# Decode attention with a gated MLP on one core: two heads side by side on the partitions, a packed P·V, and a new order of the loads

## The chip, the core and the metric

The kernel runs on one core of a Trainium2 chip (trn2). Time is device microseconds of one execution; a kernel's figure is the median of its fast runs. An execution also has a *span*, from its first to its last instruction. In nearly every run the time is some 1.8 us longer than the span (363.06 against 361.3).

## The reference, cut to what matters

```python
# B = 2 sequences, one new token each; 32 heads of 128; 4096 cached keys and values a head
q = x @ wq                                        # [2, 4096]
p = softmax(q . k_cache / sqrt(128))              # per sequence and head, over 4096 keys
o = p @ v_cache                                   # k_cache and v_cache: 67 MB each
a = o @ wo                                        # [2, 512]
b = relu(x_B @ w1) @ w2                           # w1 [512, 1376], w2 [1376, 512]
g = sigmoid((x * gate_w).sum(-1))
return g * a + (1 - g) * b
```

Every value of both caches is read once and used in two operations, so nearly all of the 145 MB that the kernel loads are K and V.

## The kernel before

The work goes in 32 steps, a step being two neighbouring heads of one sequence. A K tile has 128 partitions, and each partition holds 32 keys of the first head and then 32 of the second: two runs of 8 KB. A tile lies in SBUF, the on-chip memory. VectorE (DVE) multiplies the tile with q, TensorE (PE) sums the products in 16 matmuls with the identity, DVE finishes the sum, ScalarE (ACT) takes the exponential, and PE multiplies with V.

```python
def load_k(s):                                    # load_v is alike
    t = kpool.tile([P, 2, NC, Dh], bf16, name="kt")           # NC = 32
    nc.sync.dma_start(out=t, in_=A_k_cache[b, h : h + 2].rearrange("h (p c) d -> p h c d", p=P))
...
def pv(s):                                        # 32 matmuls, 2 output rows, 256 columns
    for c in range(NC):
        nc.tensor.matmul(o_ps, lhsT=PT_sb[:, c, 2 * s : 2 * s + 2], rhs=vt[:, :, c, :], ...)
...
def epi(s):                                       # scale, two transposes, and for b = 1 two matmuls with wo
    ...
for s in range(NP + 2):                           # NP = 32
    if s < NP: mult(s)
    if s >= 2: epi(s - 2)
    if s < NP: red(s)
    if 1 <= s <= NP: scores(s - 1); pv(s - 1)
    if s == 14: mlp()
    ...                                           # wq, wo (by quarters), w1 at s = 5, w2 at s = 7
    load_k(s + 3)
    load_v(s + 2)
res = g * a_ps + b2                               # then one output load
```

The softmax here doesn't subtract the row's maximum and nothing guards it: scores larger than these inputs give would overflow.

## Time and profile before

| | before |
|---|---|
| time, median (15 runs) | 363.59 us (361.99 to 365.68) |
| profiled run: time, span | 366.02 us, 364.2 us |
| loaded | 145.43 MB in 24,628 packets of the load queue |
| PE / DVE / ACT busy | 286.8 / 168.1 / 48.3 us |

### The profile page before, as it was taken

The page shows a single profiled execution, that of the slowest core. Times are in us where ns is not written, and L with a number is a line of the kernel's source. Part 1 is how long each engine was busy: PE and PEld are TensorE (multiplying, and loading weights), DVE is VectorE, ACT ScalarE, POOL GpSimd, SP SyncE. Part 2 cuts the span into 40 slices and gives each one's busy share as a digit, 9 for nine tenths or more (in the row PEclk, how much of TensorE's full clock was granted, in tenths as well). Part 3 has the DMA queues.
Part 4 walks back from the last instruction along what each step waited for, and adds up shares of the span by engine and source line. Part 5 has one row for each costly group of instructions (what it writes and reads, how often), then busy time and mean ns, then how long its engine had stood idle before and what let it go on. Part 6 is the DMA issues. An engine that isn't in the chain of part 4 may idle for free.

```text
span 364.2 us, 4195 instructions
## 1 busy us (share of the span) xinstructions
PE 286.8 (79%) x1812; PEld 152.6 (42%) x1815; DVE 168.1 (46%) x106; ACT 48.3 (13%) x212; POOL 0.7 (0%) x6
## 2 busy tenths in 40 slices
PE   0597977697888498469958989988979989958895
PEld 0143544253444154325614455544424455524443
DVE  0565551455451555135065555555505556455500
ACT  1201110012111011001021111111021111111011
POOL 0000000000000000000000000000000000000000
PEclk9988988699999699969899999999899999989989
DMA  7999999999999999999999999999999999999920
GB/s 253 426 426 428 429 407 426 430 426 427 427 431 405 426 426 410 429 426 427 426 428 420 404 420 417 401 427 428 426 430 426 425 428 425 416 427 425 421 94 0
DMA packets 24927, 145.70 MB, mean 400 GB/s; under 512 B 1511, under 2 KB 5709, under 8 KB 8525
## 3 DMA queue, kind: packets, MB, share of 16 engines
q1 hardware_dynamic: 24628, 145.43, 96.0%
q8 instruction: 14, 0.23, 0.2%
q10 hardware_dynamic: 280, 0.01, 0.0%
q14 instruction: 5, 0.03, 0.0%
HBM read 145.43 MB, written 0.00 MB: 399 GB/s over the span
## 4 chain that ended last, share of the span: by engine, by line
PE 40%; DMA 38%; DVE 16%; ACT 3%; SPq 1%; issue 1%; DVEq 0%; ACTq 0%
DMA kt<-in_A_k_cache_dram 38%; PE red L178 22%; DVE prod L171 15%; PE o_ps L211 11%; PE mm L153 2%; PE a_ps L233 2%; ACT qb L160 1%; ACT o L223 1%; PE mm L287 1%; PE mm L273 1%; PE gs L202 1%; PE tr L226 1%; ACT OT_sb L229 0%; SPq L320 0%; SPq L324 0%
## 5 line engine op out<-in xcount | busy, mean ns | idle before, releaser
L171 DVE TENSOR_TENSOR prod<-kt,qb 128x8192 bf16<-128x8192 bf16 x32 | 141.5, 4421 | 37.1 <-DMA kt<-in_A_k_cache_dram 36.7
L178 PE MATMUL red<-prod,ident 128*128 128x512 bf16 x512 | 131.2, 416 | 33.3 <-DVE prod L171 33.3
L211 PE MATMUL o_ps<-vt,PT_sb 128*2 128x256 bf16 x1024 | 116.9, 272 | 0.0
L178 PEld LDWEIGHTS <-ident 128*128 128x128 bf16 x512 | 52.8, 105 | 104.7 <-issue 60.1
L211 PEld LDWEIGHTS <-PT_sb 128*2 128x2 bf16 x1024 | 83.9, 84 | 24.3
L206 DVE RECIPROCAL rsg<-gs 2x1 f32<-2x1 f32 x32 | 5.0, 155 | 137.8 <-PE gs L202 137.8
L223 ACT ACTIVATE o<-o_ps,rsg 2x256 bf16<-2x256 f32 x32 | 14.8, 464 | 191.4 <-PE o_ps L211 191.4
L153 PE MATMUL mm<-wq,xb 128*128 128x512 bf16 x61 | 17.5, 403 | 17.3 <-DMA wq<-in_A_wq_dram 8.2
L192 ACT ACTIVATE PT_sb<-sc 128x32 bf16<-128x32 f32 x64 | 17.8, 338 | 54.7 <-DVE sc L190 54.7
L190 DVE TENSOR_REDUCE sc<-red 128x64 f32<-128x512 f32 x32 | 21.8, 681 | 0.6 <-PE red L178 0.6
L226 PE MATMUL tr<-ident,o 2*128 2x2 bf16 x64 | 6.3, 165 | 19.6 <-ACT o L223 19.6
L153 PEld LDWEIGHTS <-xb 128*128 128x128 bf16 x64 | 6.3, 101 | 27.5 <-issue 19.2
L226 PEld LDWEIGHTS <-o 2*128 2x128 bf16 x64 | 3.5, 92 | 29.5 <-ACT o L223 29.5
L160 ACT CAST qb<-mm 128x512 bf16<-128x512 f32 x16 | 9.4, 585 | 42.9 <-PE mm L153 42.9
L192 ACT ACTIVATION_READ_ACCUMULATOR PT_sb<-sc 128x1 f32 x64 | 13.5, 212 | 0.0
L233 PE MATMUL a_ps<-wo,OT_sb 128*2 128x512 bf16 x32 | 9.5, 377 | 4.0 <-ACT OT_sb L229 4.0
L202 PEld LDWEIGHTS gs<-ones_col,partials 128*2 128x2 f32 x64 | 2.8, 82 | 13.5 <-issue 13.1
L229 ACT COPY OT_sb<-tr 128x2 bf16<-128x2 bf16 x32 | 5.2, 163 | 9.3 <-PE tr L226 9.3
L202 PE MATMUL gs<-ones_col,partials 128*2 128x1 f32 x64 | 6.1, 164 | 0.0
L294 DVE TENSOR_SCALAR b<-mm,omg 2x512 f32<-2x512 f32 x1 | 0.7, 737 | 10.5 <-PE mm L287 10.5
L287 PE MATMUL mm<-w_sb,hT 128*2 128x512 bf16 (+1 forms) x11 | 4.2, 562 | 0.3 <-ACT hT L282 0.3
L233 PEld LDWEIGHTS <-OT_sb 128*2 128x2 bf16 x32 | 1.4, 81 | 5.5 <-ACT OT_sb L229 5.5
(21 smaller groups left out, 12.0 us busy)
## 6 DMA issues: line engine op xcount, KB each, us to landing
kt<-in_A_k_cache_dram SPq DMA_DIRECT2D x32, 2048.0 KB, 22.8
vt<-in_A_v_cache_dram SPq DMA_DIRECT2D x31, 2048.0 KB, 22.2
wq<-in_A_wq_dram SPq DMA_DIRECT2D x4, 1024.0 KB, 14.0
wo<-in_A_wo_dram SPq DMA_DIRECT2D x4, 1024.0 KB, 19.4
w_sb<-in_B_w_dram SPq DMA_DIRECT2D x1, 1376.0 KB, 28.9
w_sb<-in_B_w_dram SPq DMA_DIRECT2D x1, 1280.0 KB
vt<-in_A_v_cache_dram SPq DMA_DIRECT2D x1, 1024.0 KB, 14.6
vt<-in_A_v_cache_dram SPq DMA_DIRECT2D x2, 512.0 KB, 15.9
```

Of the source, the lines that this page charges most:

```text
L153: nc.tensor.matmul(ps, lhsT=xb[:, b, c, :], rhs=wq[:, c, n0 : n0 + 512], start=(c == 0), stop=(c == DC - 1),)
L160: nc.scalar.copy(out=qb[:, b, n0 : n0 + 512], in_=ps)
L171: nc.vector.tensor_tensor(out=prod, in0=kt, in1=q, op=ALU.mult)
L178: nc.tensor.matmul(ps, lhsT=ident, rhs=prod[:, :, j * RW : (j + 1) * RW], start=(j == 0), stop=(j == Dh // RW - 1),)
L190: nc.vector.reduce_sum(out=sc, in_=ps, axis=AX.X)
L192: nc.scalar.activation(out=PT_sb[:, :, 2 * s + i], in_=sc[:, i * NC : (i + 1) * NC], func=ACT.Exp, scale=inv_sqrt_dh, accum_out=partials[: ...
L202: nc.tensor.matmul(gs, lhsT=partials[:, 2 * s : 2 * s + 2], rhs=ones_col, start=True, stop=True)
L211: nc.tensor.matmul(o_ps, lhsT=PT_sb[:, c, 2 * s : 2 * s + 2], rhs=vt[:, :, c, :], start=(c == 0), stop=(c == NC - 1),)
L223: nc.scalar.activation(out=o4, in_=o_t.pop(s), func=ACT.Copy, scale=rsg_t.pop(s))
L226: nc.tensor.transpose(tr[:, 2 * i : 2 * i + 2], o4[:, i * Dh : (i + 1) * Dh], ident[:2, :2])
L233: nc.tensor.matmul(a_ps, lhsT=OT_sb[:, hh, :], rhs=wo[:, hh - g * GH, :], start=(hh == 0), stop=(hh == H - 1),)
L287: nc.tensor.matmul(b_ps, lhsT=hT[:fs, fc, :], rhs=w2_sb[:fs, fc, :], start=(fc == 0), stop=(fc == FC - 1),)
```

## The change

Its intent: larger pieces for the load engines, fewer and wider matmuls for P·V, and loads at the very end that nothing long has to wait for. The two heads of a step now lie side by side on the partitions (64 each), so a partition holds 64 keys of one head, one run of 16 KB. Four chunks of 128 values go into one P·V matmul with 8 output rows, and four small matmuls with a selection matrix combine them. K is loaded two steps ahead of V where it was one, the first K comes ahead of wq, and the last quarter of wo and all of w2 come last. The gate is now multiplied in earlier, so that attention and MLP add up in one accumulator, `a_ps`.

```diff
-        t = kpool.tile([P, 2, NC, Dh], bf16, name="kt")
-            out=t, in_=A_k_cache[b, h : h + 2].rearrange("h (p c) d -> p h c d", p=P)
+        return cache[b, h : h + 2].rearrange("h (p c) d -> (h p) c d", p=HP)      # kv_view, HP = 64
+        t = kpool.tile([P, NC, Dh], bf16, name="kt")                              # NC = 64
+        nc.sync.dma_start(out=t, in_=kv_view(A_k_cache, s))
...                                               # wo in 8 KB rows, wq in two loads of 4 KB rows
-        for c in range(NC):
-            nc.tensor.matmul(o_ps, lhsT=PT_sb[:, c, 2 * s : 2 * s + 2], rhs=vt[:, :, c, :], ...)
+        for q in range(NQ):                       # NQ = 16, JB = 4
+            nc.tensor.matmul(o_ps, lhsT=PT_sb[:, s % PT_SLOTS, q * JB : (q + 1) * JB, :] ...,
+                             rhs=vt[:, q * JB : (q + 1) * JB, :], ...)
...                                               # sums, evac, comb, unpack, wo_mm in place of epi
+        if 2 <= s < NP + 2:
+            pv(s - 2)
+        if s == NP + 2:
+            mlp_o()                               # the MLP's 11 output matmuls, into the same a_ps
...
-        load_v(s + 2)
+        load_v(s + 1)
+        if s + 1 == NP - 1:
+            load_wo(NG - 1)
+            load_w2()
```

More of the change, by code (lines that the diff above doesn't have):

```diff
@@ L17 @@
 RW = 8
+JB = 4
+PT_SLOTS = 4
 @with_exitstack
@@ L45 @@
     P = nc.NUM_PARTITIONS
+    HP = P // 2
     assert Dh == P
     DC = D // P
-    NC = Sk // P
-    BH = B * H
-    NP = BH // 2
+    NC = Sk // HP
+    NQ = NC // JB
+    M = 2 * JB
+    NP = B * H // 2
     NG = H // GH
-    PPG = B * GH // 2
+    GP = GH // 2
+    PPG = B * GP
+    DR = GH * Dh // P
+    DA = Dh // DR
+    WQG = 2
     inv_sqrt_dh = 1.0 / (float(Dh) ** 0.5)
@@ L59, in pair @@
         g, r = divmod(s, PPG)
-        b, r = divmod(r, GH // 2)
-        return g, b, g * GH + 2 * r
+        b, i = divmod(r, GP)
+        return g, b, i
     consts = ctx.enter_context(tc.tile_pool(name="consts", bufs=1))
@@ L69 @@
     qbpool = ctx.enter_context(tc.tile_pool(name="qbpool", bufs=2))
-    smalls = ctx.enter_context(tc.tile_pool(name="smalls", bufs=4))
+    smalls = ctx.enter_context(tc.tile_pool(name="smalls", bufs=3))
     PS = bass.MemoryType.PSUM
@@ L74 @@
     mmp = ctx.enter_context(tc.tile_pool(name="mmp", bufs=1, space=PS))
-    trp = ctx.enter_context(tc.tile_pool(name="trp", bufs=1, space=PS))
+    combp = ctx.enter_context(tc.tile_pool(name="combp", bufs=1, space=PS))
     gsp = ctx.enter_context(tc.tile_pool(name="gsp", bufs=1, space=PS))
@@ L81, with load_wq, kv_view @@
     wq_view = A_wq.rearrange("(p c) n -> p c n", c=DC)
-    wo_view = A_wo.rearrange("(h p) j -> p h j", p=P)
     wq_t, qb_t, wo_t, k_t, v_t = {}, {}, {}, {}, {}
-    def load_wq(g):
-        t = wqpool.tile([P, DC, GH * Dh], bf16, name="wq")
-        nc.sync.dma_start(out=t, in_=wq_view[:, :, g * GH * Dh : (g + 1) * GH * Dh])
-        wq_t[g] = t
-    def load_wo(g):
-        t = wopool.tile([P, GH, D], bf16, name="wo")
-        nc.sync.dma_start(out=t, in_=wo_view[:, g * GH : (g + 1) * GH, :])
+    def load_wq(i):
+        w = WQG * GH * Dh
+        t = wqpool.tile([P, DC, w], bf16, name="wq")
+        nc.sync.dma_start(out=t, in_=wq_view[:, :, i * w : (i + 1) * w])
+        wq_t[i] = t
+    def load_wo(g):
+        t = wopool.tile([P, DR, D], bf16, name="wo")
+        rows = GH * Dh
+        nc.sync.dma_start(
+            out=t, in_=A_wo[g * rows : (g + 1) * rows].rearrange("(p r) j -> p r j", r=DR)
+        )
         wo_t[g] = t
+    def kv_view(cache, s):
+        g, b, i = pair(s)
+        h = g * GH + 2 * i
+        return cache[b, h : h + 2].rearrange("h (p c) d -> (h p) c d", p=HP)
     def load_k(s):
@@ L98, in load_k @@
             return
-        _, b, h = pair(s)
-        t = kpool.tile([P, 2, NC, Dh], bf16, name="kt")
-        nc.sync.dma_start(
-            out=t, in_=A_k_cache[b, h : h + 2].rearrange("h (p c) d -> p h c d", p=P)
-        )
+        t = kpool.tile([P, NC, Dh], bf16, name="kt")
+        nc.sync.dma_start(out=t, in_=kv_view(A_k_cache, s))
         k_t[s] = t
@@ L108, in load_v @@
             return
-        _, b, h = pair(s)
-        t = vpool.tile([P, 2, NC, Dh], bf16, name="vt")
-        view = A_v_cache[b, h : h + 2].rearrange("h (p c) d -> p h c d", p=P)
-        cuts = [0, NC] if s < NP - 1 else [0, NC // 2, 3 * NC // 4, NC]
+        t = vpool.tile([P, NC, Dh], bf16, name="vt")
+        view = kv_view(A_v_cache, s)
+        cuts = [0, NC] if s < NP - 1 else [0, NC // 2, NC]
         for c0, c1 in zip(cuts, cuts[1:]):
-            nc.sync.dma_start(out=t[:, :, c0:c1, :], in_=view[:, :, c0:c1, :])
+            nc.sync.dma_start(out=t[:, c0:c1, :], in_=view[:, c0:c1, :])
@@ L115, in load_v @@
         v_t[s] = t
+    pad = consts.tile([P, 32], bf16, name="pad")
+    nc.gpsimd.memset(pad, 0.0)
+    load_k(0)
     xT = consts.tile([P, B, DC], bf16, name="xT")
-    nc.scalar.dma_start(out=xT, in_=A_x[:, 0, :].rearrange("b (p c) -> p b c", c=DC))
+    nc.sync.dma_start(out=xT, in_=A_x[:, 0, :].rearrange("b (p c) -> p b c", c=DC))
+    gwT = consts.tile([P, DC], bf16, name="gwT")
+    nc.sync.dma_start(out=gwT, in_=gate_w.rearrange("(p c) -> p c", c=DC))
     load_wq(0)
-    x_sb = consts.tile([B, D], bf16, name="x_sb")
@@ L121 @@
-    nc.scalar.dma_start(out=x_sb, in_=A_x[:, 0, :])
-    gw_sb = consts.tile([B, D], bf16, name="gw_sb")
-    nc.scalar.dma_start(out=gw_sb, in_=gate_w.partition_broadcast(B))
-    load_k(0)
     load_k(1)
+    load_k(2)
     load_v(0)
-    load_k(2)
-    load_v(1)
     ident = consts.tile([P, P], bf16, name="ident")
     make_identity(nc, ident[:])
-    ones_col = consts.tile([P, 1], fp32, name="ones_col")
-    nc.vector.memset(ones_col, 1.0)
-    PT_sb = consts.tile([P, NC, BH], bf16, name="PT_sb")
@@ L135 @@
-    partials = consts.tile([P, BH], fp32, name="partials")
-    OT_sb = consts.tile([P, H, B], bf16, name="OT_sb")
+    sel = consts.tile([M, JB, 32], bf16, name="sel")
+    nc.gpsimd.memset(sel, 0.0)
+    nc.gpsimd.affine_select(
+        out=sel,
+        in_=sel,
+        compare_op=ALU.not_equal,
+        fill=1.0,
+        base=0,
+        pattern=[[-2, JB], [-1, 2], [0, DA]],
+        channel_multiplier=1,
+    )
+    half = consts.tile([P, M], fp32, name="half")
+    nc.vector.memset(half, 0.0)
@@ L137 @@
+    nc.vector.memset(half[:HP, 0::2], 1.0)
+    nc.vector.memset(half[HP:, 1::2], 1.0)
+    PT_sb = consts.tile([P, PT_SLOTS, NC, 2], bf16, name="PT_sb")
+    nc.vector.memset(PT_sb, 0.0)
+    umask = consts.tile([P, DA], fp32, name="umask")
+    nc.vector.reduce_sum(
+        out=umask, in_=ident.rearrange("p (k a) -> p a k", a=DA), axis=AX.X
+    )
+    partials = consts.tile([P, NP], fp32, name="partials")
+    OT_sb = consts.tile([P, NG, DR, B], bf16, name="OT_sb")
     w1_sb = consts.tile([P, DC, Dff], bf16, name="w1_sb")
@@ L138 @@
     w2_sb = consts.tile([P, FC, D], bf16, name="w2_sb")
-    xb = consts.tile([P, B, DC, P], bf16, name="xb")
+    xb = consts.tile([P, B, DC, HP], bf16, name="xb")
     for b in range(B):
         nc.vector.tensor_copy(
-            out=xb[:, b], in_=xT[:, b, :].unsqueeze(2).to_broadcast([P, DC, P])
+            out=xb[:, b], in_=xT[:, b, :].unsqueeze(2).to_broadcast([P, DC, HP])
         )
+    gwb = consts.tile([P, DC, P], bf16, name="gwb")
+    nc.vector.tensor_copy(out=gwb, in_=gwT.unsqueeze(2).to_broadcast([P, DC, P]))
@@ L144 @@
     a_ps = apool.tile([B, D], fp32, name="a_ps")
+    g_sb = consts.tile([P, B], fp32, name="g_sb")
+    omg = consts.tile([P, B], fp32, name="omg")
     def make_qb(g):
-        wq = wq_t.pop(g)
-        qb = qbpool.tile([P, B, GH * Dh], bf16, name="qb")
+        wq = wq_t[g // WQG].rearrange("p c (i t d) -> p c t i d", t=2, d=Dh)
+        i0 = (g % WQG) * GP
+        qb = qbpool.tile([P, B, GP, Dh], bf16, name="qb")
         for b in range(B):
-            for n0 in range(0, GH * Dh, 512):
-                ps = mmp.tile([P, 512], fp32, name="mm")
+            ps = mmp.tile([P, GP * Dh], fp32, name="mm")
+            for t in range(2):
@@ L152, in make_qb @@
                 for c in range(DC):
                     nc.tensor.matmul(
-                        ps,
+                        ps[t * HP : (t + 1) * HP, :],
                         lhsT=xb[:, b, c, :],
-                        rhs=wq[:, c, n0 : n0 + 512],
+                        rhs=wq[:, c, t, i0 : i0 + GP, :],
                         start=(c == 0),
@@ L159, in make_qb @@
                     )
-                nc.scalar.copy(out=qb[:, b, n0 : n0 + 512], in_=ps)
+            nc.scalar.copy(out=qb[:, b], in_=ps.rearrange("p (i d) -> p i d", d=Dh))
         qb_t[g] = qb
-    prod_t, red_t, o_t, o4_t, rsg_t = {}, {}, {}, {}, {}
+    prod_t, red_t, o_t, osb_t, rsg_t, comb_t = {}, {}, {}, {}, {}, {}
     def mult(s):
-        g, b, h = pair(s)
-        kt = k_t.pop(s)
-        q = qb_t[g][:, b, (h - g * GH) * Dh : (h - g * GH + 2) * Dh]
-        q = q.rearrange("p (h d) -> p h d", h=2).unsqueeze(2).to_broadcast([P, 2, NC, Dh])
-        prod = prodpool.tile([P, 2, NC, Dh], bf16, name="prod")
-        nc.vector.tensor_tensor(out=prod, in0=kt, in1=q, op=ALU.mult)
+        g, b, i = pair(s)
+        q = qb_t[g][:, b, i, :].unsqueeze(1).to_broadcast([P, NC, Dh])
+        prod = prodpool.tile([P, NC, Dh], bf16, name="prod")
+        nc.vector.tensor_tensor(out=prod, in0=k_t.pop(s), in1=q, op=ALU.mult)
         prod_t[s] = prod
     def red(s):
-        prod = prod_t.pop(s).rearrange("p h c d -> p (h c) d")
-        ps = redp.tile([P, 2 * NC, RW], fp32, name="red")
+        prod = prod_t.pop(s)
+        ps = redp.tile([P, NC, RW], fp32, name="red")
         for j in range(Dh // RW):
@@ L187, in scores @@
     def scores(s):
-        ps = red_t.pop(s)
-        sc = smalls.tile([P, 2 * NC], fp32, name="sc")
-        nc.vector.reduce_sum(out=sc, in_=ps, axis=AX.X)
-        for i in range(2):
+        sc = smalls.tile([P, NC], fp32, name="sc")
+        nc.vector.reduce_sum(out=sc, in_=red_t.pop(s), axis=AX.X)
+        for t in range(2):
+            r = slice(t * HP, (t + 1) * HP)
             nc.scalar.activation(
-                out=PT_sb[:, :, 2 * s + i],
-                in_=sc[:, i * NC : (i + 1) * NC],
+                out=PT_sb[r, s % PT_SLOTS, :, t],
+                in_=sc[r],
@@ L195, in scores, with sums @@
                 func=ACT.Exp,
                 scale=inv_sqrt_dh,
-                accum_out=partials[:, 2 * s + i : 2 * s + i + 1],
+                accum_out=partials[r, s : s + 1],
             )
-    def pv(s):
-        gs = gsp.tile([2, 1], fp32, name="gs")
-        nc.tensor.matmul(
-            gs, lhsT=partials[:, 2 * s : 2 * s + 2], rhs=ones_col, start=True, stop=True
-        )
-        rsg = smalls.tile([2, 1], fp32, name="rsg")
-        nc.vector.reciprocal(out=rsg, in_=gs)
-        rsg_t[s] = rsg
+    def sums(s):
+        gs = gsp.tile([M, 1], fp32, name="gs")
+        nc.tensor.matmul(gs, lhsT=half, rhs=partials[:, s : s + 1], start=True, stop=True)
+        rsg = smalls.tile([M, 1], fp32, name="rsg")
+        nc.vector.reciprocal(out=rsg, in_=gs)
+        b = pair(s)[1]
+        nc.vector.tensor_tensor(out=rsg, in0=rsg, in1=g_sb[:M, b : b + 1], op=ALU.mult)
+        rsg_t[s] = rsg
@@ L208, in pv @@
+    def pv(s):
         vt = v_t.pop(s)
-        o_ps = opool.tile([2, 2 * Dh], fp32, name="o_ps")
-        for c in range(NC):
+        o_ps = opool.tile([M, JB * Dh], fp32, name="o_ps")
+        for q in range(NQ):
             nc.tensor.matmul(
                 o_ps,
-                lhsT=PT_sb[:, c, 2 * s : 2 * s + 2],
-                rhs=vt[:, :, c, :],
-                start=(c == 0),
-                stop=(c == NC - 1),
+                lhsT=PT_sb[:, s % PT_SLOTS, q * JB : (q + 1) * JB, :].rearrange(
+                    "p j t -> p (j t)"
+                ),
+                rhs=vt[:, q * JB : (q + 1) * JB, :],
+                start=(q == 0),
+                stop=(q == NQ - 1),
@@ L217, in pv @@
             )
         o_t[s] = o_ps
-    def epi(s):
-        g, b, h = pair(s)
-        o4 = smalls.tile([2, 2 * Dh], bf16, name="o4")
-        nc.scalar.activation(out=o4, in_=o_t.pop(s), func=ACT.Copy, scale=rsg_t.pop(s))
-        tr = trp.tile([P, 4], bf16, name="tr")
-        for i in range(2):
-            nc.tensor.transpose(
-                tr[:, 2 * i : 2 * i + 2], o4[:, i * Dh : (i + 1) * Dh], ident[:2, :2]
-            )
-        nc.scalar.copy(out=OT_sb[:, h : h + 2, b], in_=tr[:, 0:4:3])
-        if b == B - 1:
-            wo = wo_t[g]
-            for hh in (h, h + 1):
-                nc.tensor.matmul(
-                    a_ps,
-                    lhsT=OT_sb[:, hh, :],
-                    rhs=wo[:, hh - g * GH, :],
-                    start=(hh == 0),
-                    stop=(hh == H - 1),
-                )
@@ L241, with evac @@
-    g_sb = consts.tile([B, 1], fp32, name="g_sb")
-    omg = consts.tile([B, 1], fp32, name="omg")
-    b2 = consts.tile([B, D], fp32, name="b2")
-    def gate():
-        gtmp = consts.tile([B, D], bf16, name="gtmp")
-        gz = consts.tile([B, 1], fp32, name="gz")
-        nc.vector.tensor_tensor_reduce(
-            out=gtmp,
-            in0=x_sb,
-            in1=gw_sb,
-            scale=1.0,
-            scalar=0.0,
-            op0=ALU.mult,
-            op1=ALU.add,
-            accum_out=gz,
-        )
-        ge = consts.tile([B, 1], fp32, name="ge")
-        nc.scalar.activation(out=ge, in_=gz, func=ACT.Exp, scale=-1.0)
+    def evac(s):
+        osb = smalls.tile([M, JB, Dh], bf16, name="osb")
+        nc.scalar.activation(
+            out=osb,
+            in_=o_t.pop(s).rearrange("m (j d) -> m j d", d=Dh),
+            func=ACT.Copy,
+            scale=rsg_t.pop(s),
+        )
+        osb_t[s] = osb
@@ new lines, in comb, with unpack @@
+    def comb(s):
+        g, b, i = pair(s)
+        if i == 0:
+            comb_t[g, b] = combp.tile([P, Dh], fp32, name="comb")
+        ps = comb_t[g, b]
+        osb = osb_t.pop(s)
+        for j in range(JB):
+            nc.tensor.matmul(
+                ps[32 * i : 32 * (i + 1), :],
+                lhsT=sel[:, j, :],
+                rhs=osb[:, j, :],
+                start=(j == 0),
+                stop=(j == JB - 1),
+            )
+    def unpack(s):
+        g, b, i = pair(s)
+        if i != GP - 1:
+            return
+        ps = comb_t.pop((g, b)).rearrange("p (a r) -> p r a", r=DR)
+        tmp = smalls.tile([P, DR, DA], fp32, name="tmp")
+        nc.vector.tensor_tensor(
+            out=tmp, in0=ps, in1=umask.unsqueeze(1).to_broadcast([P, DR, DA]), op=ALU.mult
+        )
+        with nc.allow_low_precision("o is rounded to bf16 once, as the reference does"):
+            nc.vector.reduce_sum(out=OT_sb[:, g, :, b], in_=tmp, axis=AX.X)
@@ new lines, in wo_mm @@
+    def wo_mm(s):
+        g, b, i = pair(s)
+        if i != GP - 1 or b != B - 1:
+            return
+        wo = wo_t.pop(g)
+        for r in range(DR):
+            nc.tensor.matmul(
+                a_ps,
+                lhsT=OT_sb[:, g, r, :],
+                rhs=wo[:, r, :],
+                start=(g == 0 and r == 0),
+                stop=(g == NG - 1 and r == DR - 1),
+            )
+    def gate():
+        ps = mmp.tile([P, GP * Dh], fp32, name="mm")
+        z = ps[:, :B]
+        for c in range(DC):
+            nc.tensor.matmul(
+                z, lhsT=gwb[:, c, :], rhs=xT[:, :, c], start=(c == 0), stop=(c == DC - 1)
+            )
+        ge = consts.tile([P, B], fp32, name="ge")
+        nc.scalar.activation(out=ge, in_=z, func=ACT.Exp, scale=-1.0)
@@ L262, in gate, with mlp_h @@
         nc.vector.tensor_scalar(omg, g_sb, -1.0, 1.0, op0=ALU.mult, op1=ALU.add)
-    def mlp():
-        hT = consts.tile([P, FC, B], bf16, name="hT")
-        ps = mmp.tile([P, 512], fp32, name="mm")
+    hT = consts.tile([P, B, FC], bf16, name="hT")
+    def mlp_h():
+        ps = mmp.tile([P, GP * Dh], fp32, name="mm")
         h_ps = ps[:, : FC * B].rearrange("p (f b) -> p f b", b=B)
@@ L271, in mlp @@
             for c in range(DC):
-                lhsT = w1m[:, c, fc, :] if fc < FF else w1_sb[:, c, FF * P :]
                 nc.tensor.matmul(
                     h_ps[:fs, fc, :],
-                    lhsT=lhsT,
+                    lhsT=w1m[:, c, fc, :] if fc < FF else w1_sb[:, c, FF * P :],
                     rhs=xT[:, :, c],
@@ L279, in mlp @@
                 )
-        nc.scalar.activation(out=hT[:, :FF, :], in_=h_ps[:, :FF, :], func=ACT.Relu)
-        if FREM:
-            nc.scalar.activation(out=hT[:FREM, FF, :], in_=h_ps[:FREM, FF, :], func=ACT.Relu)
-        ps2 = mmp.tile([P, 512], fp32, name="mm")
-        b_ps = ps2[:B, :D]
-        for fc in range(FC):
-            fs = P if fc < FF else FREM
-            nc.tensor.matmul(
-                b_ps,
-                lhsT=hT[:fs, fc, :],
-                rhs=w2_sb[:fs, fc, :],
-                start=(fc == 0),
-                stop=(fc == FC - 1),
+        for b in range(B):
+            nc.scalar.activation(
+                out=hT[:, b, :FF], in_=h_ps[:, :FF, b], func=ACT.Relu, scale=omg[:, b : b + 1]
+            )
+            if FREM:
+                nc.scalar.activation(
+                    out=hT[:FREM, b, FF:],
+                    in_=h_ps[:FREM, FF:, b],
+                    func=ACT.Relu,
+                    scale=omg[:FREM, b : b + 1],
+                )
@@ new lines, with load_w2, mlp_o @@
+    W2_CUTS = [0, 4, 8, FF]
+    def load_w2():
+        if FREM:
+            nc.sync.dma_start(out=w2_sb[:FREM, FF, :], in_=B_w2[FF * P :, :])
+        view = B_w2[: FF * P].rearrange("(p f) j -> p f j", f=FF)
+        for f0, f1 in zip(W2_CUTS, W2_CUTS[1:]):
+            nc.sync.dma_start(out=w2_sb[:, f0:f1, :], in_=view[:, f0:f1, :])
+    def mlp_o():
+        order = ([FF] if FREM else []) + list(range(FF))
+        for f in order:
+            fs = P if f < FF else FREM
+            nc.tensor.matmul(
+                a_ps,
+                lhsT=hT[:fs, :, f],
+                rhs=w2_sb[:fs, f, :],
+                start=False,
+                stop=False,
@@ L293, in mlp @@
             )
-        nc.vector.tensor_scalar(b2, b_ps, omg, None, op0=ALU.mult)
     make_qb(0)
-    for s in range(NP + 2):
+    for s in range(NP + 4):
         if s < NP:
             mult(s)
-        if s >= 2:
-            epi(s - 2)
+        if s >= 4:
+            unpack(s - 4)
+        if 3 <= s < NP + 2:
+            sums(s - 2)
+        if 3 <= s < NP + 3:
+            evac(s - 3)
         if s < NP:
             red(s)
+            if s >= 3:
+                comb(s - 3)
         if 1 <= s <= NP:
@@ L305 @@
             scores(s - 1)
-            pv(s - 1)
         if s == 1:
             gate()
+        if s == 2:
+            sums(0)
+        if 2 <= s < NP + 2:
+            pv(s - 2)
+        if s == NP + 2:
+            mlp_o()
+        if NP <= s < NP + 3:
+            comb(s - 3)
+        if s >= 4:
+            wo_mm(s - 4)
         if s == 14:
-            mlp()
+            mlp_h()
         if s % PPG == PPG - 2 and (s + 2) // PPG < NG:
             make_qb((s + 2) // PPG)
-        if s % PPG == 2 and (s // PPG) + 1 < NG:
-            load_wq(s // PPG + 1)
@@ L315 @@
-        if s % PPG == 2 and s < NP:
+        if s == 9:
+            load_wq(1)
+        if s % PPG == 3 and s < NP - PPG:
             load_wo(s // PPG)
@@ L318 @@
             nc.sync.dma_start(out=w1_sb, in_=B_w1.rearrange("(p c) f -> p c f", c=DC))
-        if s == 7:
-            nc.sync.dma_start(
-                out=w2_sb[:, :FF, :], in_=B_w2[: FF * P].rearrange("(p f) j -> p f j", f=FF)
-            )
-            if FREM:
-                nc.sync.dma_start(out=w2_sb[:FREM, FF, :], in_=B_w2[FF * P :, :])
         load_k(s + 3)
-        load_v(s + 2)
+        load_v(s + 1)
+        if s + 1 == NP - 1:
+            load_wo(NG - 1)
+            load_w2()
     res = consts.tile([B, D], bf16, name="res")
-    nc.vector.scalar_tensor_tensor(
-        out=res, in0=a_ps, scalar=g_sb, in1=b2, op0=ALU.mult, op1=ALU.add
-    )
+    nc.vector.tensor_copy(out=res[:, : D // 2], in_=a_ps[:, : D // 2])
+    nc.scalar.copy(out=res[:, D // 2 :], in_=a_ps[:, D // 2 :])
     nc.sync.dma_start(out=out[:, 0, :], in_=res)
```

## The prediction

> **What bounds the kernel now.** I read the page first: engines, then the slices, then the chain.
>
> ```profile
> span 364.2 us, 4195 instructions
> PE 286.8 (79%) x1812; PEld 152.6 (42%) x1815; DVE 168.1 (46%) x106; ACT 48.3 (13%) x212; POOL 0.7 (0%) x6
> ...
> GB/s 253 426 426 428 429 407 426 430 426 427 427 431 405 426 426 410 429 426 427 426 428 420 404 420 417 401 427 428 426 430 426 425 428 425 416 427 425 421 94 0
> ...
> q1 hardware_dynamic: 24628, 145.43, 96.0%
> ```
>
> No engine is full, but the load queue is: 145.43 MB at about 428 GB/s for 36 of 40 slices. At 428 GB/s the bytes alone take 339.8 us. The rest is at three places: a slow first slice, dips to 401-420, and two last slices with almost no loads. The windows view shows the two ends, in the columns window, PE, PEld, DVE, ACT, POOL busy, granted clock, DMA share and GB/s:
>
> ```profile
> 2.00:4.00 2.00, 0.00 (x0) 0.10 (x1) 0.76 (x2) 1.28 (x1) 0.00 (x0) 1.00 0.81 182
> 4.00:6.00 2.00, 0.00 (x0) 0.00 (x0) 0.00 (x0) 0.00 (x0) 0.00 (x0) 1.00 1.01 322
> 6.00:8.00 2.00, 0.00 (x0) 0.00 (x0) 0.00 (x0) 0.00 (x0) 0.00 (x0) 1.00 1.02 396
> 280.00:290.00 10.00, 9.14 (x61) 4.84 (x60) 5.11 (x3) 1.20 (x6) 0.00 (x0) 1.00 1.02 428
> 346.00:348.00 2.00, 2.00 (x7) 0.73 (x6) 0.15 (x1) 0.56 (x4) 0.00 (x0) 0.56 0.81 317
> 348.00:350.00 2.00, 2.00 (x7) 0.74 (x6) 0.00 (x0) 0.00 (x0) 0.00 (x0) 0.59 0.26 99
> 350.00:352.00 2.00, 2.00 (x18) 1.11 (x16) 0.74 (x2) 0.00 (x0) 0.00 (x0) 1.00 0.05 15
> ```
>
> Loads start at 2 us, and half-microsecond windows show the last bytes at 350.5. I read the fall from 347 on as some of the 16 engines being done, the slowest at 350.5. What follows is bare compute, in the timeline (start, length, what):
>
> ```profile
> 341.12 4.43 DVE L171 TENSOR_TENSOR prod<-kt,qb 128x8192 bf16<-128x8192 bf16 x1 [1.33 <-DMA kt<-in_A_k_cache_dram]
> 345.60 5.30 PE L178 MATMUL red<-prod,ident 128*128 128x512 bf16 x16 [0.89 <-DVE prod L171]
> 350.89 3.65 PE L211 MATMUL o_ps<-vt,PT_sb 128*2 128x256 bf16 x32
> 356.05 3.65 PE L211 MATMUL o_ps<-vt,PT_sb 128*2 128x256 bf16 x32
> 361.34 0.74 DVE L329 SCALAR_TENSOR_TENSOR res<-a_ps,g_sb,b 2x512 bf16<-2x512 f32 x1 [4.96 <-PE a_ps L233]
> ```
>
> The last K lands at 341.1, and everything done with it is 23.1 us long while only about 9 us of loads are left to hide it. So the kernel is load-bound from 2 to 350.5 and has 13.7 us of tail. The chain of waits agrees: 38% of it is the K load, and from 341 on it is PE and DVE.
>
> **What the Trainium skill says.** "DMA: Bandwidth & Descriptors", Why small descriptors are slow: a fixed cost per packet inside the engine. I grouped the trace's packet records by size: median 46 ns for 1 KB, 84 for 2 KB, 159 for 4 KB, 309 for 8 KB, 385 for 10 KB, 413 for 11 KB. From 4 to 8 KB that is 36.6 ps a byte, with some 9 ns left over for each packet; the trace agrees with the idea. Same page, Where 436 GB/s comes from: a ceiling of 435.2 GB/s. Our 428 is below it, so about 1.7% can be won there at most on K and V. "TensorE: Matmul & The Clock Gate", Back-to-back issue gap: time goes with the moving columns, about N/2.4 + 2.5 ns, not with output rows. The trace agrees: 16 matmuls of 512 columns take 3.56 us (222 ns each), 32 of 256 take 3.53 us (110 ns each). Same page, Part 1: The HAM clock gate: PE idle for microseconds falls to half clock. The windows show 0.56 at 346-348, and there red took 5.30 us instead of 3.56.
>
> **The change part by part.**
> *P·V packing.* The 1024 matmuls of 256 columns become 512 of 512 columns, with 8 output rows: the same 8192 columns a pair, so 3.55 us a pair as before. The two small transposes and two output matmuls a pair go, with their stalls on ACT (19.6 us and 4.0 us of idle PE in the groups); four 128-column combining matmuls come (estimate 0.3 us). PE needs about 7.8 us a pair against 8.8 before. A pair's loads, 4.19 MB, take 9.8 us, so this saving lies beside the loads and is worth nothing in the middle.
> *DVE, ACT.* Multiply and reduction keep their sizes (4.42 + 0.68 us); nothing there nears 9.8 us.
> *Packets.* A K or V tile is now one run of 16 KB in each partition instead of two of 8 KB; wo goes from 1 KB to 8 KB, wq from 2 to 4 KB, w2 from 10 KB to 4, 4 and 2 KB. I take a 16 KB packet as 309 + 8192 x 36.6 ps = 609, say 610 ns. Saved, on each of 16 engines: K and V 8064 pairs of packets x (618 - 610) / 16 = 4.0 us; wo (4096 x 46 - 512 x 309) / 16 = 1.9 us; wq (2048 x 84 - 1024 x 159) / 16 = 0.6 us; w2 loses 0.1. Sum 6.4 us, all on the bound.
> *Start.* K0 goes first, in large packets, and wq second. Between 2 and 8 us the loads moved 1.8 MB where 428 GB/s would give 2.57: 1.8 us lost. I count 0.6 us of it as won. The first multiply moves from 13 to about 17-18 us, but three K, one V and wq (10.5 MB, until about 26 us) are queued by then, so the engines do not run dry.
> So the last byte comes at 350.5 - 7.0 = 343.5 us.
> *The order of the end.* V is now loaded one pair later, and wo's last part and all of w2 come last of all. After the last K there are V29, V30, V31, wo and w2: 8.75 MB, 20.4 us. The last K is then there at 343.5 - 20.4 = 323.1 us. From it runs the PE path: multiply 4.43, red 3.6 to 5.3 (4.6), three P·V 10.65, sums and combining 0.9, the 11 MLP matmuls 11 x 0.222 + 0.2 = 2.6, last combining 0.35, the two unpacking steps 0.55, the 8 output matmuls 7 x 0.222 + 0.377 = 1.9, the copy of half a row 0.45, the output DMA 2.1 (before: 362.1 to 364.2), handovers 0.5: 29.0 us, so 352.1. The other path, from the last byte of w2, is 2 MLP matmuls 0.6 and the same steps after it, about 6.4 us: 349.9. The later one counts, unless the clock is full and PE is a little quicker. I say 351.5: 12 us less, some 7 from the loads and 5 from the tail.
>
> **Rivals.**
> *The packets gain nothing*: something else than the packet holds the loads at 428. For it: 428 is already close to the skill's ceiling, packets overlap (the DMA share reads 1.01 to 1.02), and a dip to 375 at 200-204 us has no small packets in it. Against: the 10 and 11 KB packets follow the same line. Then only the tail is won: 350.5 - 20.4 + 29.0 = 359, within 2%.
> *PE becomes the bound or goes cold.* At half clock (weight loads 0.43 us apart at 347-349 us) a pair's 32 large matmuls cost some 14 us, over the 9.8. For it: more idle PE between pairs. Against: before, idle PE was followed by catching up with the DMA share still 1.01, and some 15 us of loads are queued when a V buffer comes free. It would add 1 to 4 us, mostly at the end, where the PE path decides.
> *V's later load starves the queue.* V(s+1) waits for P·V(s-2), about 12 us after K(s) lands; at that time V(s-1), K(s+2), V(s) and K(s+3) are still to come, some 17 us. I expect no gap. If there were one, each pair would lose some tenths and all would be back at 360.
> *The tail is hidden wholly*: the last byte sets the end, 349 to 350.
>
> **Range and chances.** Packets as worked out and the end as summed: 351.5. Packets worth half, or a cold end: 354 to 356. All as hoped: 347 to 349. The 2% line is 356.3. So 346.5 to 356.5; faster 0.85, within 2% 0.14, slower 0.01.
>
> **What would show it.** Right: some 12,000 fewer packets; slices at 431-433 GB/s and shallower dips; the last bytes near 343 and under 10 us of span after them; PE busy near 265 us; K waits at multiply in nearly every pair. Wrong: 8 KB packets or slices still at 428; DMA share well under 1 in the middle (starved); PE waiting for w2 long after its other work (then loads, not PE, set the end); red or P·V at twice their time in the tail.

## The result, and the profile after

| | before | after |
|---|---|---|
| time, median | 363.59 us (15 runs) | 353.54 us (353.27 to 355.79, 9 runs) |
| profiled run: time, span | 366.02, 364.2 us | 354.90, 353.1 us |
| packets of the load queue | 24,628 | 12,100 |

The ratio is 0.9742, 95% interval 0.972 to 0.9764: faster. (A ratio is the mean time of one kernel's runs over that of the other's of the same rounds, so it is not quite the ratio of the medians.) The medians differ by 10.0 us. Executions over 1.5% slower than the fastest of the same kernel are left out of the means.

The page of the kernel after:

```profile
span 353.1 us, 3330 instructions
PE 284.5 (81%) x1371; PEld 119.5 (34%) x1371; DVE 175.0 (50%) x156; ACT 50.7 (14%) x175; POOL 1.2 (0%) x9
...
GB/s 276 432 444 419 442 419 440 421 430 437 424 436 427 418 433 440 419 440 425 434 427 436 420 438 429 429 429 434 431 429 432 429 431 429 436 423 440 417 304 0
...
q1 hardware_dynamic: 12100, 145.43, 97.0%
```

The same bytes in half the packets. Busy PE hardly fell (286.8 to 284.5 us). The slices between the first and the last with loads swing between 417 and 444, so the middle is better read as one window of 300 us. This is the windows view of the kernel before and then of the kernel after (columns as in the prediction; the DMA share is the summed duration of the packets over the time of the 16 load engines, and it passes 1.00 where packets overlap):

```profile
20.00:320.00 300.00, 246.61 (x1585) 132.68 (x1587) 143.78 (x90) 39.41 (x181) 0.00 (x0) 0.94 1.01 423
```

```profile
20.00:320.00 300.00, 253.39 (x1223) 107.04 (x1223) 162.01 (x134) 43.83 (x159) 0.00 (x0) 0.93 1.01 430
340.00:342.00 2.00, 2.00 (x15) 0.81 (x14) 0.30 (x2) 0.68 (x1) 0.00 (x0) 1.00 0.92 341
342.00:344.00 2.00, 2.00 (x11) 0.82 (x10) 0.00 (x0) 0.00 (x0) 0.00 (x0) 1.00 0.28 110
344.00:346.00 2.00, 2.00 (x13) 0.73 (x11) 0.00 (x0) 0.68 (x1) 0.00 (x0) 1.00 0.03 8
```

The rate rises from 423 to 430 GB/s, and the last bytes of the loads come at 344.0 us where they came at 350.5. (What the window from 344 still moves is one 16 KB packet of PE's instructions; the expectations below, which count it, say 344.5.) Both kernels keep the load engines full: the DMA share is 1.01 in both. The waits view says the same from DVE's side, first before, then after (who waited for whom: total us, times, longest):

```profile
DVE prod L171 <- DMA kt<-in_A_k_cache_dram: 36.7, 13, 9.7
```

```profile
DVE prod L203 <- DMA kt<-in_A_k_cache_dram: 107.8, 24, 8.8
```

DVE waits three times as long for K and it costs nothing: compute now runs ahead of the loads and stands at the next K. Waiting time of an engine that does not set the end is no loss.

The end, in the timeline of the kernel after:

```profile
323.55 4.42 DVE L203 TENSOR_TENSOR prod<-kt,qb 128x8192 bf16<-128x8192 bf16 x1 [4.51 <-DMA kt<-in_A_k_cache_dram]
...
328.02 5.17 PE L210 MATMUL red<-prod,ident 128*128 128x512 bf16 x16 [2.27 <-DVE prod L203]
...
333.45 3.62 PE L245 MATMUL o_ps<-vt,PT_sb 128*8 128x512 bf16 x16
...
340.88 3.61 PE L245 MATMUL o_ps<-vt,PT_sb 128*8 128x512 bf16 x16
...
344.74 2.54 PE L361 MATMUL a_ps<-w_sb,hT 96*2 96x512 bf16 x11
...
348.31 1.89 PE L299 MATMUL a_ps<-wo,OT_sb 128*2 128x512 bf16 x8 [0.71 <-DVE OT_sb L291]
350.24 0.41 DVE L414 CAST res<-a_ps 2x256 bf16<-2x256 f32 x1 [1.98 <-PE a_ps L299]
```

The last K is there at 323.55 us, 17.6 us earlier than before: 6.5 us because the loads end earlier, and 11 because 20.4 us of other loads follow it (8.75 MB) in place of 9.4. From there PE never waits for a load: when it comes to the MLP matmuls at 344.74, w2 has just landed. The path from the last K to the end is 29.6 us. Its one oddity is the sum of products (red), 5.17 us in place of 3.61: at its start, from 328 to 330 us, the windows view gives a granted clock of 0.50 (the share of full speed that TensorE got). Of the nine runs, five had spans of 351.5 to 351.8 us and four of 352.3 to 353.9; the profiled one is among the slower four.

### The profile page after: what moved, and what is told of

It is laid out like the page before. It is cut to its first block, busy times and chain, and to the rows that moved or that the text cites. A ratio compares the mean times of both kernels' runs of the same rounds, so it can differ in the third digit from the quotient of the medians.

```text
span 353.1 us, 3330 instructions
## 1 busy us (share of the span) xinstructions
PE 284.5 (81%) x1371; PEld 119.5 (34%) x1371; DVE 175.0 (50%) x156; ACT 50.7 (14%) x175; POOL 1.2 (0%) x9
## 3 DMA queue, kind: packets, MB, share of 16 engines
q1 hardware_dynamic: 12100, 145.43, 97.0%
## 4 chain that ended last, share of the span: by engine, by line
DMA 56%; PE 28%; DVE 14%; ACT 1%; SPq 0%; issue 0%; DVEq 0%
DMA kt<-in_A_k_cache_dram 53%; PE red L210 13%; DVE prod L203 12%; PE o_ps L245 10%; DMA wq<-in_A_wq_dram 3%; PE mm L187 2%; PE comb L273 1%; PE mm L329 1%; PE a_ps L361 1%; PE a_ps L299 1%; ACT qb L194 0%; DVE sc L221 0%; PE gs L234 0%; DVE rsg L236 0%; SPq L135 0%
## 5 line engine op out<-in xcount | busy, mean ns | idle before, releaser
L245 PE MATMUL o_ps<-vt,PT_sb 128*8 128x512 bf16 x512 | 115.6, 379 | 0.0
L245 PEld LDWEIGHTS <-PT_sb 128*8 128x8 bf16 x512 | 41.9, 87 | 60.8
L258 ACT ACTIVATE osb<-o_ps,rsg 8x512 bf16<-8x512 f32 x32 | 21.7, 677 | 179.6 <-PE gs L234 156.0
L224 ACT ACTIVATE PT_sb<-sc 64x64 bf16<-64x64 f32 x64 | 17.5, 274 | 64.4 <-DVE sc L221 64.0
L187 PE MATMUL mm<-wq,xb 128*64 128x512 bf16 x64 | 12.0, 505 | 17.5 <-DMA wq<-in_A_wq_dram 14.0
L273 PE MATMUL comb<-osb,sel 8*32 8x128 bf16 x128 | 12.5, 217 | 0.0
L224 ACT ACTIVATION_READ_ACCUMULATOR PT_sb<-sc 64x1 f32 x64 | 11.8, 185 | 0.0
L273 PEld LDWEIGHTS <-sel 8*32 8x32 bf16 x128 | 7.0, 91 | 13.6 <-issue 13.2
L234 PEld LDWEIGHTS gs<-partials,half 128*8 128x8 f32 x64 | 5.3, 90 | 9.0 <-issue 1.6
L234 PE MATMUL gs<-partials,half 128*8 128x1 f32 x64 | 6.1, 165 | 0.0
```

Of the source, the lines that this page charges most:

```text
L187: nc.tensor.matmul(ps[t * HP : (t + 1) * HP, :], lhsT=xb[:, b, c, :], rhs=wq[:, c, t, i0 : i0 + GP, :], start=(c == 0), stop=(c == DC - 1),)
L224: nc.scalar.activation(out=PT_sb[r, s % PT_SLOTS, :, t], in_=sc[r], func=ACT.Exp, scale=inv_sqrt_dh, accum_out=partials[r, s : s + 1],)
L234: nc.tensor.matmul(gs, lhsT=half, rhs=partials[:, s : s + 1], start=True, stop=True)
L245: nc.tensor.matmul(o_ps, lhsT=PT_sb[:, s % PT_SLOTS, q * JB : (q + 1) * JB, :].rearrange("p j t -> p (j t)"), rhs=vt[:, q * JB : (q + 1) * ...
L258: nc.scalar.activation(out=osb, in_=o_t.pop(s).rearrange("m (j d) -> m j d", d=Dh), func=ACT.Copy, scale=rsg_t.pop(s),)
L273: nc.tensor.matmul(ps[32 * i : 32 * (i + 1), :], lhsT=sel[:, j, :], rhs=osb[:, j, :], start=(j == 0), stop=(j == JB - 1),)
```

## The experiments

All kernels gave the right result. Each was timed in three rounds and profiled once. Figures are medians; "the changed kernel" is 353.54 us. It was not run again beside the experiments, which came on three chips. The kernel before was, and the medians there are 363.1, 363.5 and 362.9 us, so a difference under 1 us means little by its size alone.

**1. K and V in 8 KB packets again.** A gap in the middle of each partition of the tile breaks the run on the SBUF side; bytes, loads and compute stay.

```diff
-        t = kpool.tile([P, NC, Dh], bf16, name="kt")
-        nc.sync.dma_start(out=t, in_=kv_view(A_k_cache, s))
+        t = kpool.tile([P, 2, NC // 2 + 1, Dh], bf16, name="kt")[:, :, : NC // 2, :]
+        nc.sync.dma_start(out=t, in_=kv_view(A_k_cache, s).rearrange("p (u c) d -> p u c d", u=2))
```

> The changed kernel with a gap in the middle of each partition of the K and V tiles, so that their loads fall into 8 KB packets again; bytes, order and all compute the same. Packet theory (some 9 ns for each packet, 16 KB at 611 ns and 8 KB at 309 ns in the trace): 8064 packets more at (618 - 611) / 16 to (618 - 610) / 16 ns, 3.5 to 4.0 us on every load engine, last byte near 348, time 357 to 357.6. Rival, packets gain nothing and the win came from the order of the end alone: 353.5, last byte near 344.5.

Measured: 356.12 us, 2.6 us slower. The windows view:

```profile
20.00:320.00 300.00, 250.12 (x1214) 106.10 (x1214) 160.42 (x131) 43.26 (x155) 0.00 (x0) 0.92 1.01 427
```

427 GB/s in place of 430, the last K at 326.3 in place of 323.55. So packets do count, against the rival, but for two thirds of what I had worked out. The packet records of the trace tell why: 8 KB takes 309 ns and 16 KB takes 611 ns in the median, just as assumed, yet the packets' durations add up to 1.011 of the 16 engines' time in this window and to 1.008 in the changed kernel. Packets overlap a little, and the small ones overlap more. Of the 1.1% that a merged pair saves (7 ns in 618), 0.3% were hidden already; what remains, 0.8% of about 340 us, is some 2.7 us, near the 2.6 measured. (This is bookkeeping of the same trace, not a second test.)

**2. wo and wq in small packets as well.**

```diff
-        t = wopool.tile([P, DR, D], bf16, name="wo")
+        t = wopool.tile([P, DR, D + 64], bf16, name="wo")[:, :, :D]            # 1 KB runs
-        t = wqpool.tile([P, DC, w], bf16, name="wq")
+        t = wqpool.tile([P, DC, 2, w // 2 + 64], bf16, name="wq")              # 2 KB runs
```

> As the run before it, and wo in 1 KB and wq in 2 KB packets again. Packet theory: 1.9 us for wo and 0.6 us for wq on top, 6.0 to 6.5 us in all against the changed kernel: 359.5 to 360. If only the small packets matter: about 356, with the 8 KB run unchanged. If packets gain nothing: 353.5.

Measured: 357.60 us, 1.5 us more than the run before and 4.1 us more than the changed kernel. The window of 20 to 320 us is at 426 GB/s. Both kinds of packet count; the whole is 4.1 us where I had 6.4.

**3. w2 and the last wo quarter early.**

```diff
-        if s % PPG == 3 and s < NP - PPG:
+        if s % PPG == 3 and s < NP:
             load_wo(s // PPG)
...
-        if s + 1 == NP - 1:
-            load_wo(NG - 1)
+        if s == 7:
             load_w2()
```

> The changed kernel with the last quarter of wo and all of w2 loaded in the middle, as before the change, and not after the last V. Theory (the compute chain from the last K, 29.6 us in the changed kernel's trace, sets the end): only V29, V30 and V31 (6.3 MB, 14.7 us) follow the last K, which then lands at 344.5 - 14.7 = 329.8 us; end 329.8 + 29.6 = 359.4, so 359.5 to 360, 6 us slower. Rival (the last byte sets the end): P.V of the last half 1.9, then MLP, combining, output as before: about 355.

Measured: 359.66 us, 6.1 us slower, and the four runs lie within 0.7 us. Its timeline:

```profile
329.58 4.42 DVE L203 TENSOR_TENSOR prod<-kt,qb 128x8192 bf16<-128x8192 bf16 x1 [4.43 <-DMA kt<-in_A_k_cache_dram]
...
334.06 3.61 PE L210 MATMUL red<-prod,ident 128*128 128x512 bf16 x16 [0.66 <-DVE prod L203]
...
354.71 0.41 DVE L413 CAST res<-a_ps 2x256 bf16<-2x256 f32 x1 [1.98 <-PE a_ps L299]
```

The last K comes 6.0 us later (329.8 had been worked out) and the end moves with it. From the last K to the end of the span (357.6) it takes 28.0 us here, with red at its full 3.61 us. That is the length of the path in an undisturbed run; the changed kernel's median agrees: 323.55 + 28.0 = 351.6 us of span, and 1.8 us make 353.4.

**4. The MLP matmuls last.** `mlp_o()` issued after `wo_mm(31)` and not ahead of the last combining.

> The changed kernel with the 11 MLP output matmuls issued after the last output matmuls and not before the last combining. Theory (PE's own work from the last K sets the end, w2 is there in time): no gain, rather 0.7 us more because the last combining now waits for ACT's copy of P.V (0.68 us) that the MLP matmuls used to cover: 353.5 to 354.3. Rival (the last byte of w2 at 344.5 sets the end and what follows it is the delay): combining, unpacking and 8 output matmuls would come ahead of the wait, 2.5 us gained: 351.

Measured: 355.17 us (353.98 to 357.16, so a noisy set; two of the four times are 2.5 and 3.5 us over their spans), the fastest run 0.7 us slower than the changed kernel's fastest, and so by span (352.2 against 351.5). Nothing is gained, so the last byte of w2 is not what holds the end by itself: PE's own work is.

**5. and 11. P·V with 256 columns.** `JB = 4` becomes `JB = 2`, nothing else in the source: as many P·V matmuls as before the change. It was run on other chips.

> The changed kernel with JB = 2: P.V in 32 matmuls of 256 columns with 4 output rows (as many as before the change) in place of 16 of 512 with 8, and two combining matmuls a pair in place of four. Theory (a pair's loads take 9.7 us and PE has slack; moving columns, not output rows or instructions, cost PE time): within 0.5 us of the changed kernel, 353.5. Rival (the packing is what freed PE and so the loads): 2 us or more slower.

> JB = 2 once more, in another call and another place in it. If the 2.7 us belong to the kernel: 356 again, all packets about 0.5% longer than in the changed kernel (614 against 611 ns). If they came from that call's chip or placement: 353.5 and 611 ns.

Measured: 356.24 and 356.85 us, 2.7 and 3.3 us slower: the rival's number, but not its reason. The windows view of the second of them:

```profile
20.00:320.00 300.00, 248.95 (x1599) 139.58 (x1599) 160.10 (x131) 36.96 (x154) 0.00 (x0) 0.92 1.01 427
```

The loss is in the load rate, 427 in place of 430 GB/s, with the same 12,100 packets: a 16 KB packet took 614 ns in the median of both runs where it took 611 in the changed kernel. PE was not late: busy 249 of 300 us, and the last multiply still waited 4.5 us for its K. So the loads themselves are slower.

The matmuls of P·V are not what starts it. The first of them starts at 39.8 us (41.0 in the second run), and until then the engines do the same work as in the changed kernel, but for the filling of two small constants and the row sums of the first step. The packet records show most of the loss already there. From 12 us to the first P·V matmul a 16 KB packet took 614.9 ns in the mean (613.7 in the second run), and 611 in the changed kernel, in every one of 715; from there to 320 us it took 615.5 in both runs, and 611.9 in the changed kernel.

JB changes something else, which the source hardly shows. `sel`, the selection matrix, has 256 bytes in each partition with JB = 4 and 128 with JB = 2, so all tiles allocated behind it move. Both kernels were built once more to read the addresses: with JB = 2 all K, V, wq and wo tiles start 128 bytes earlier (the first K buffer at byte 43,904 and not 44,032), so that none lies at a multiple of 256 bytes any more. Before the change, in the changed kernel and in experiments 1, 3, 9 and 12 all of them do, and there 98% or more of the K and V packets between 20 and 320 us have one and the same duration; with JB = 2, 24% at most. That makes the address the first suspect. It is not shown: the w1 tile lies off such multiples in the changed kernel too, and its packets keep to one duration (413 ns in 98% of them).

**9. As many PE instructions, but tiny ones.** The next suspect was the instruction stream. The queue table of the page (packets, MB, share) shows PE's program coming over the same load engines, 11 packets of 16 KB in the changed kernel and 14 with JB = 2:

```diff
         nc.tensor.matmul(gs, lhsT=half, rhs=partials[:, s : s + 1], start=True, stop=True)
+        for _ in range(14):
+            nc.tensor.matmul(gs2[:1, 1:2], lhsT=ident[:, :1], rhs=ident[:, :1], start=True, stop=True)
```

> The changed kernel with 14 one-column matmuls (and their weight loads) a pair more on PE, some 0.6 us of PE a pair, which has 2 us of idle there. PE's program then has 3544 rows, as many as the kernel with JB = 2, and as the trace shows for that one its instructions should come in 14 packets of 16 KB over the same load engines instead of 11. Theory (the 2.7 us that JB = 2 cost are instruction fetches or the number of PE instructions): 356 as well. Rival (it was the shape of P.V, or nothing that the kernel does): 353.5.

```profile
q8 instruction: 14, 0.23, 0.2%
```

Measured: 354.20 us, 0.7 us slower, at 430 GB/s and 611 ns a packet, although the 14 packets are there (the line above is from its page). Neither instruction fetches nor the number of PE instructions explain JB = 2. What does is open. The shift of the tiles is the nearest rival; JB = 2 with `sel` padded to its old size would test it, and no such run was made.

**6. The start as before:** wq ahead of the first K, x and the gate vector on ACT's queue.

```diff
-    load_k(0)
-    nc.sync.dma_start(out=xT, in_=...)
+    nc.scalar.dma_start(out=xT, in_=...)
     ...
     load_wq(0)
+    load_k(0)
```

> The changed kernel with the start as before: xT and the gate vector on the ACT queue, wq ahead of the first K on the SP queue. Theory: the start is worth little, some 0.5 us: 353.5 to 354. Rival (the first K in front is what fills the first slice): the first slice falls back towards 253 GB/s and the time rises by 1 us or more.

Measured: 353.53 us, no difference. From 2 to 8 us this one moves 362 GB/s, the changed kernel 326, the kernel before 300. The first K in front wins nothing. What sets these three rates apart is not shown: wq's packets, the small loads and their queues differ between the kernels.

**7. The last K in halves.** Two loads, two multiplies and two sums of 256 columns for step 31 alone.

```diff
+    def halves(s):
+        return [(0, NC)] if s < NP - 1 else [(0, NC // 2), (NC // 2, NC)]
...
-        nc.sync.dma_start(out=t, in_=kv_view(A_k_cache, s))
+        for c0, c1 in halves(s):
+            nc.sync.dma_start(out=t[:, c0:c1, :], in_=view[:, c0:c1, :])
...                                               # mult and red alike
```

> The changed kernel with the last K pair in two halves (two loads, two multiplies, two reductions of 256 columns). Theory (the compute chain from the last K sets the end, the loads' last byte is close behind): PE gets 4 us ahead, so w2's last byte at 344.5 takes over as the bound, and 6.6 us of steps follow it: span 351.1, 0.5 us under an undisturbed run of the changed kernel (span 351.6, time 353.5), so 353.0, and without the runs near 355. If the chain alone counted: 350.

Measured: 353.04 us (352.88 to 353.53), as worked out, though 0.5 us is no more than calls differ by; experiment 6, of the same call, is at 353.53. The trace is the better evidence. PE is ahead now and its MLP matmuls stand waiting for w2 in three pieces:

```profile
342.18 0.38 PE L369 MATMUL a_ps<-w_sb,hT 96*2 96x512 bf16 x1 [0.45 <-DMA w_sb<-in_B_w_dram]
343.27 1.02 PE L369 MATMUL a_ps<-w_sb,hT 128*2 128x512 bf16 x4 [0.72 <-DMA w_sb<-in_B_w_dram]
344.53 1.46 PE L369 MATMUL a_ps<-w_sb,hT 128*2 128x512 bf16 x6 [0.24 <-DMA w_sb<-in_B_w_dram]
```

None of the four runs is near 355.

**8. Halves, and the MLP matmuls last.** Experiments 4 and 7 together.

> The last K in halves, and the MLP matmuls last (the order that gained nothing by itself). Theory: with PE ahead, the steps behind the last byte shrink to the MLP matmuls, the copies and the output: span 349, time 350.5 to 351, 2.5 to 3 us faster than the changed kernel. Rival (neither path is what holds the end): 353.5.

Measured: 352.23 us, 1.3 us faster than the changed kernel and half of what I expected. In its timeline P·V ends at 341.5, the output matmuls start at 343.41 after two waits (0.49 us for ACT, 0.71 for DVE), and all 11 MLP matmuls (2.54 us, from 345.14) then lie behind them: PE's path was still the longer one.

**10. Both gains undone** (2 and 3 together).

> The changed kernel with both of its gains undone at once: K, V, wq and wo in small packets (4.1 us in the earlier run) and w2 and the last wo loaded early (6.1 us). If the two are the whole of the change and independent: 353.5 + 10.2 = 363.7, the kernel before. If something else of the change (packing, start, V order) gains too: under 362.

Measured: 363.72 us (363.54 to 363.95), the time of the kernel before (ratio 0.9982, interval 0.9905 to 1.006), and the sum that was expected, 363.7. Packets and late loads add up, and together they are as large as the whole gain; what else the change contains (packing, start) sums to nothing visible here.

**12. A version that beats both.** The last K in halves, w2 ahead of the last wo quarter, that quarter in two loads, two of the MLP matmuls behind the last combining, where PE waits for DVE.

```diff
-            load_wo(NG - 1)
             load_w2()
+            load_wo(NG - 1)                       # in two loads of 4 rows each
...
-            mlp_o()
+            mlp_o(0, 9)
         if NP <= s < NP + 3:
             comb(s - 3)
+        if s == NP + 2:
+            mlp_o(9, FC)
```

The result tile is also cut in two, each with its own output load.

> A candidate to beat both: the last K in halves, w2 ahead of the last wo quarter, that quarter in two loads, two MLP matmuls moved into the unpacking gap, the result in two tiles with two output loads. Theory (compute from the last K and steps behind the last byte both shortened): PE done with P.V at 341.4, output matmuls 344.5 to 346.4, copies and output 2.5 us more, span 349, time 350.5. If the loads' last byte does not matter or the end is held by something not seen: 352 to 353.

Measured: 351.73 us (350.9 to 352.74; ratio to the kernel before 0.9656, interval 0.9589 to 0.9723), 1.8 us faster than the changed kernel by the medians. Two runs had the span of 349.1 us that was worked out, two took 350.7 and 351.0. The profile is of the longest:

```profile
343.00 2.11 PE L370 MATMUL a_ps<-w_sb,hT 96*2 96x512 bf16 x9
345.03 0.39 PE L282 MATMUL comb<-osb,sel 8*32 8x128 bf16 x4
345.36 0.59 PE L370 MATMUL a_ps<-w_sb,hT 128*2 128x512 bf16 x2
...
346.13 1.89 PE L308 MATMUL a_ps<-wo,OT_sb 128*2 128x512 bf16 x8 [0.18 <-DVE OT_sb L300]
```

The gap ahead of the output matmuls has gone from 0.71 to 0.18 us, and two of the eleven MLP matmuls now run inside it, where PE had stood waiting. P·V still ended 1.3 us later than reckoned in this run, behind a red of the step before that took 5.30 us. The edits of this version were not tried one by one.

## Why the prediction was right or wrong

*The bound and the sum.* 351.5 us against 353.54 measured, a gain of 12 us against 10.0. The mechanism holds: loads bound the kernel until the last K, and PE's own path from there sets the end. The last byte was put at 343.5 us and came at 344.0, the last K at 323.1 and came at 323.55; the path was put at 29.0 us and took 29.6 in the profiled run, 28.0 undisturbed. Two things went into the 2 us. First, I rounded 352.1 down to 351.5 for a quicker PE. Second, I set the span of one profile beside the median of the times as if they were the same, though the profiled run's own time (366.02) was listed: it was a run 2.4 us above the median, and a time is 1.8 us more than its span. 351.6 us of span is 353.4 us of time.

That the last byte fell so close was in part luck. The sum began at 350.5, the last byte of that slow run, and took off 7.0 us, where the experiments find 4.1 for the packets and nothing for the start. In experiment 10, with the packet sizes of the kernel before, the loads ended at 348.5. The starting point was some 2 us late and the saving some 3 us too large, and the two nearly cancel.

*Packets ("Sum 6.4 us, all on the bound").* Right in mechanism, mis-sized. Experiments 1 and 2 give 2.6 us for K and V (4.0 reckoned) and 1.5 us for wo and wq (2.5 reckoned), together 4.1. The term that was too large is the saving for each packet, taken from durations that partly overlap. (The 1.7% given as the most to be won on K and V is an estimate from the ceiling that the prediction cites; the 427 to 430 GB/s of experiment 1 are 0.8%.) The share of over 1.00, which I had read and named in the rival, was the hint. Of the signs named, 12,528 fewer packets and 9.1 us of span after the last byte came true, and K waits in 24 of 32 pairs; the rate was 430 and not 431 to 433.

*Start ("I count 0.6 us of it as won").* Experiment 6 shows none of it for the order of the loads (it keeps the larger wq packets).

*The end ("some 7 from the loads and 5 from the tail").* The late loads are worth 6.1 us (experiment 3), more than the 5 given to the tail, so the two errors in the split made up for each other. Experiments 3, 4 and 7 show the chain as stated: the end follows the last K, does not follow the order of the MLP, and passes to w2's last byte once PE's path is cut shorter.

*P·V packing ("this saving lies beside the loads and is worth nothing in the middle").* Nothing here refutes it, and experiment 10 agrees: it has the packed P·V, with the small packets and early loads, and is no faster than the kernel before, which packs nothing. Experiments 5 and 11 were meant as the test and cannot serve as one: the packets are slow before P·V begins, and the tiles lie elsewhere. Whether 256-column P·V would cost anything with the tiles in place stays open. The working had two slips. The output matmuls do not go: both pages have 32 of them, now eight at a time. And the combining costs PE 12.5 us busy where the transposes took 6.3, so PE's busy time, expected near 265 us, is 284.5.

*The rivals.* "The packets gain nothing" fell with experiment 1. "V's later load starves the queue" fell with the DMA share of 1.01. "PE goes cold" is there in the small: 1.5 us in the profiled run. The prediction put the 5.30 us of red in the kernel before down to an idle PE, though its own line shows a gap of only 0.89 us ahead of it. "The tail is hidden wholly" fell with experiment 3, and experiment 7 shows that it takes a shorter PE path to come near it.

## What to carry to other kernels

In a load-bound kernel look at what is loaded last: put loads with little compute behind them at the end, and count the compute path from the last piece that has much. Make the runs in a partition as long as the layout allows, but take the gain from rates in a long window, not from single packets' durations. Compare times with times: check what the profiled run itself took before reading its span as typical. And when an experiment changes a constant, ask what else moves with it: here one number also shifted every tile that the loads write to, and the test no longer tested what it was made for.

## What the Trainium skill lacked or had wrong

- "DMA: Bandwidth & Descriptors", Why small descriptors are slow, gives a fixed cost per packet with a 256-byte example. The runs show that it is still to be seen from 8 to 16 KB, 427 against 430 GB/s (experiment 1), and that part of it is hidden by overlap: 2.6 us where the durations alone gave 4.0. The page has neither.
- "TensorE: Matmul & The Clock Gate", Part 1: The HAM clock gate, speaks of idle windows of about 3.4 us ahead of half clock. In the changed kernel PE had stood idle for 2.27 us, in a stretch with such a gap in every pair, and red took 5.17 us and not 3.61; in experiment 1 the gap was 2.65 us and red took 3.61, and in the kernel before 0.89 us and 5.30. The length of the one gap did not decide it, which the page's remark that the window is free-running would allow.
